# Attention, expert layer and feed-forward on one core: token lists kept in SBUF, a repriced schedule, grouped 64-token tails

## The chip, the core and the metric

One core of a Trainium2 chip runs the whole program in one launch. TensorE (PE, with its weight loads as PEld) does the matrix products, VectorE (DVE) and ScalarE (ACT) the elementwise work, GpSimd (POOL) elementwise work and the indirect DMAs, SyncE (SP) issues the plain DMAs. All DMAs share 16 DMA engines. The metric is the device time of one execution in microseconds (us), the median of three runs.

## The reference

Three stages follow each other. Every token goes to exactly one of 8 experts, 576 tokens each.

```python
# 1: attention without a token-by-token product, 8 batches, 8 heads, 576 tokens, 64 wide
q_s = softmax(q, axis=-1)              # over the 64 features
k_s = softmax(k, axis=2)               # over the 576 tokens
kv  = einsum('bhsd,bhse->bhde', k_s, v)
x   = einsum('bhsd,bhde->bhse', q_s, kv)    # -> (4608, 512)
# 2: experts; tokens are given out greedily by descending logit, at most 576 per expert
logits = x @ w_gate
out[mask_e] = relu(x[mask_e] @ w1[e]) @ w2[e]        # 512 -> 1024 -> 512
# 3: dense feed-forward, 512 -> 2048 -> 512
h = x @ w_in
y = (h * tanh(softplus(h))) @ w_out
```

## The kernel before, in words

**The planner.** Nothing here is ordered by hand. Every piece of work is given to `Sched.op` (L45) with its engine, an estimated cost, what it reads and writes, a priority (lower goes first) and the buffers it takes. `Sched.run` (L75) plays this forward and emits, again and again, the piece that could start first by those costs, ties going to the priority. What comes out is a fixed order of instructions on each engine; each engine works through its own in order, so an instruction that waits holds up everything behind it on that engine. There are four such plans: attention with the first routing, the expert phases, the last pieces of the last expert, and the feed-forward.

**Attention** (L137 to L479). Per batch, `k_side` takes the maximum of k over the tokens, POOL subtracts it (`sub`, `subh`) and ACT takes the exponential. `kv_side` multiplies k by v into one PSUM tile: `mm` (L295) runs, per head, four matmuls over 128 tokens (L304) and one over the last 64 (L308). `norm` (L312) sums two columns (L315), adds a small constant (L316), inverts and scales. `q_side` does the same for q, multiplies it with kv, forms the gate logits (L397 to L402), and scales x, mostly on POOL (`late`, L409). `store` writes x to the DRAM tensor `xd`.

**Routing** (`route`, L569, `round`, L774). For each expert in turn, six rounds of comparing on DVE (`cm`, L790) and counting on PE (`rt`, L798) find the threshold; `rows` writes the weight row numbers `wi`; `onehot` and `lists` then gather the 576 token numbers, and `ids` writes them to the SBUF tile `ix` (L755). `keep` (L760) copies them to a DRAM list `gl` with two DMAs of 4-byte elements (L763, L764). Much later `ldg` (L1278) reads all lists back as `gix`, by which the feed-forward scatters its output rows.

**Expert phases.** `load_x` (L877) gathers the tokens by `ix` with five indirect DMAs from POOL (`xg`, L883), PE transposes them (`tp`, `tpf`), ACT and DVE split them into a high and a low part `xT`. `load_expert` (L847) gathers the weights in eight indirect DMAs of 512 KB (`wst`, three buffers, L855), and ACT and DVE split each into two `unit` tiles (L836, L842). `expert` (L916) then runs 128 groups of three matmuls for `hp` (L925) and `yp` (L942) per expert. Interleaved are the routing of the next expert and `convert_w` (L997): 32 blocks of the feed-forward weights are read (SP), rebuilt (ACT, DVE) and written back to DRAM as `wd`. Its first seven blocks may start when the first list is known (L1050).

**Feed-forward** (L1104): `hp` (L1115) and `yp` (L1157) over nine chunks of 512 tokens.

Of the kernel before, what the change touches and what calls it, by code (L numbers as in the profile page):

```python
# [12 lines left out]
I32 = mybir.dt.int32  # L13
# [123 lines left out]
def attention(tc, nc, cst, q, k, v, w_gate, xs, L, R, xd, route):  # L137
# [27 lines left out]
    def load_k(b):  # L165
# [10 lines left out]
        for blk in range(2):  # L176
            sc.op("DMA", 1.46, lambda blk=blk: one_blk(blk), w=[("k", b, blk)] + ([("kk", b)] if blk == 0 else []),
                  new=[("k", ("kk", b))] if blk == 0 else [], prio=0)
        if b % 2 == 0:
            sc.op("DMA", 1.46, half, w=[("kh", b // 2)], new=[("kh", ("kh", b // 2))], prio=0)  # L180

    def load_v(b):
# [10 lines left out]
        for blk in range(2):  # L193
            sc.op("DMA", 1.46, lambda blk=blk: one_blk(blk), w=[("v", b, blk)] + ([("vv", b)] if blk == 0 else []),
                  new=[("v", ("vv", b))] if blk == 0 else [], prio=0)
        if b % 2 == 0:
            sc.op("DMA", 1.46, half, w=[("vh", b // 2)], new=[("vh", ("vh", b // 2))], prio=0)

    def load_q(b):
# [10 lines left out]
        for blk in range(2):  # L210
            sc.op("DMA", 1.46, lambda blk=blk: one_blk(blk), w=[("q", b, blk)], new=[("q", ("q", b, blk))], prio=0)
        if b % 2 == 1:
            sc.op("DMA", 1.46, half, w=[("q", b, 2)], new=[("qh", ("q", b, 2))], prio=0)


    def k_side(b):
# [58 lines left out]
        sc.op(DVE, 0.6, lambda: mx1(0), r=[("k", b, 0), kk], w=[km], new=[("km", km)], prio=p)  # L275
        sc.op(DVE, 1.2, lambda: mx1(1), r=[("k", b, 1), kk], w=[km], prio=p)
        sc.op(DVE, 0.6, mx2, r=[kh, km], w=[km, khx], prio=p)
        sc.op(PE, 0.45, tr, r=[km], w=[mT], new=[("mT", mT)], prio=p)
        sc.op(DVE, 0.65, red, r=[mT], w=[dg], new=[("dg", dg)], prio=p)
        sc.op(PE, 0.45, bc, r=[dg], w=[mb], new=[("mT", mb)], prio=p)  # L280
        sc.op(ACT, 0.5, cp, r=[mb], w=[ms], new=[("ms", ms)], prio=p)
        for blk in range(2):
            sc.op(POOL, 2.3, lambda blk=blk: sub(blk), r=[ms, kk, ("k", b, blk)], w=[("k", b, blk)], prio=p)
            sc.op(ACT, 0.95, lambda blk=blk: ex(blk), r=[kk], w=[("k", b, blk)], prio=p)
        sc.op(POOL, 1.2, subh, r=[ms, kh, khx], w=[khx], prio=p)
        sc.op(ACT, 0.52, exh, r=[kh], w=[khx], prio=p)


    def kv_side(b):
# [5 lines left out]
        def mm(h0, h1):  # L295
            if h0 == 0:
                T[kvp] = ps.tile([128, 4, 66], F32, name="kvp", tag="mT", bufs=2)
            pt = T[kvp]
            for h in range(h0, h1):
                a, i = h % 2, h // 2  # L300
                n = 0
                for blk in range(2):
                    for r in range(2):
                        nc.tensor.matmul(pt[a * 64:a * 64 + 64, i, r:r + 65], T["k", b, blk][:, h, r, :],  # L304
                                         T["v", b, blk][:, h, 65 * r:65 * r + 65],
                                         start=(h == a and n == 0), stop=False, skip_group_check=True)
                        n += 1
                nc.tensor.matmul(pt[a * 64:a * 64 + 64, i, 1:66], T["kh", b // 2][o:o + 64, h, :],  # L308
                                 T["vh", b // 2][o:o + 64, h, :], start=False, stop=(h >= 6),
                                 skip_group_check=True)  # L310
# [26 lines left out]
        def cpg():  # L337
            nc.scalar.activation(kv[:, :, 128:144], T[g], AF.Copy)

        kr = [("k", b, 0), ("k", b, 1), ("khx", b), ("kh", b // 2), ("kk", b), ("vv", b), ("v", b, 0),  # L340
              ("v", b, 1), ("vh", b // 2)]
        for h0 in range(0, 8, 4):
            sc.op(PE, 0.9, lambda h0=h0: mm(h0, h0 + 4), r=kr, w=[kvp],
                  new=[("mT", kvp)] if h0 == 0 else [], prio=p)
        sc.op(DVE, 1.3, norm, r=[kvp], w=[KVk], new=[("KV", KVk)], prio=p)
        sc.op(PE, 0.45, tr, r=[KVk], w=[kT], new=[("mT", kT)], prio=p)
        sc.op(ACT, 0.5, cp, r=[kT], w=[kTs], prio=p)
        sc.op(PE, 0.9, gate, r=[kTs], w=[g], new=[("mT", g)], prio=p)
        sc.op(ACT, 0.1, cpg, r=[g], w=[KVk], prio=p)


    def q_side(b):
# [78 lines left out]
        for u in range(2 + b % 2):  # L431
            n = 1 if u == 2 else 2
            qk, m, qe = ("q", b, u), ("qm", b, u), ("qe", b, u)
            sc.op(DVE, 0.06 + 0.53 * n, lambda u=u: mx(u), r=[qk], w=[m], prio=p)
            sc.op(POOL, 0.1 + 0.9 * n, lambda u=u: sub(u), r=[m], w=[qk], prio=p)
            sc.op(ACT, 0.1 + 0.43 * n, lambda u=u: ex(u), r=[qk], w=[qe], new=[("qe", qe)], prio=p)
            for r in range(n):
                qT, xp, x = ("qT", b, u, r), ("xp", b, u, r), ("x", b, u, r)
                sc.op(PE, 0.45, lambda u=u, r=r: tr(u, r), r=[qe], w=[qT], new=[("qT", qT)], prio=p)
                sc.op(ACT, 0.5, lambda u=u, r=r: cp(u, r), r=[qT], w=[x], prio=p)  # L440
                sc.op(PE, 1.0, lambda u=u, r=r: mm(u, r),
                      r=[x, ("KV", b)] + ([("KV", b - 1)] if u == 2 else []), w=[xp],
                      new=[("xp", xp)], prio=p)
                sc.op(DVE, 0.55, lambda u=u, r=r: logits(u, r), r=[xp], w=[("R", b, u, r), ("L", j_of(u) + r)],
                      prio=p + 3.11)
                if (j_of(u) + r) % 6 < 5 or b == 7 and u == 2:
                    sc.op(ACT, 0.5, lambda u=u, r=r: copy(u, r), r=[xp], w=[x], prio=p + 3.74)
                    sc.op(POOL, 1.25, lambda u=u, r=r: late(u, r), r=[("R", b, u, r)], w=[x], prio=1000)
                else:
                    sc.op(DVE, 0.62, lambda u=u, r=r: out(u, r), r=[xp, ("R", b, u, r)], w=[x], prio=p + 3.74)  # L450

            sc.op("DMA", 0.73 * n, lambda u=u: store(u), r=[("x", b, u, r) for r in range(n)], prio=3000)
# [106 lines left out]
class Moe:  # L559


    def __init__(self, tc, nc, c, L, sm):
# [770 lines left out]
```

## Time and profile before

| what | value |
|---|---|
| median of three runs | 1568.68 us (1568.53 to 1569.06) |
| the profiled execution: its time, its span | 1567.17 us, 1565.4 us |
| mean granted PE clock | 0.968 |
| busy: PE, DVE, ACT, POOL | 93%, 62%, 48%, 18% |
| DMA | 161.03 MB, mean 103 GB/s |

The span runs from the first to the last instruction that the profiler saw. PE is busy almost all the time, but that is a mean over stages: a table of stretches shows for each how long PE worked and which clock it was granted (1.00 is 2.4 GHz, 0.50 is 1.2 GHz). A timeline row gives the start, the duration, the instruction and, in brackets, how long the engine stood idle before it and what ended that. For a DMA the profile gives the time from its issue to its landing.

### The profile page before, as it was taken

The page shows a single profiled execution, that of the slowest core. Times are in us where ns is not written, and L with a number is a line of the kernel's source. Part 1 is how long each engine was busy: PE and PEld are TensorE (multiplying, and loading weights), DVE is VectorE, ACT ScalarE, POOL GpSimd, SP SyncE. Part 2 cuts the span into 40 slices and gives each one's busy share as a digit, 9 for nine tenths or more (in the row PEclk, how much of TensorE's full clock was granted, in tenths as well). Part 3 has the DMA queues.
Part 4 walks back from the last instruction along what each step waited for, and adds up shares of the span by engine and source line. Part 5 has one row for each costly group of instructions (what it writes and reads, how often), then busy time and mean ns, then how long its engine had stood idle before and what let it go on. Part 6 is the DMA issues. An engine that isn't in the chain of part 4 may idle for free.

```text
span 1565.4 us, 24440 instructions
## 1 busy us (share of the span) xinstructions
PE 1459.3 (93%) x9698; PEld 1269.4 (81%) x9698; DVE 968.2 (62%) x2017; ACT 747.2 (48%) x1334; POOL 284.2 (18%) x302
## 2 busy tenths in 40 slices
PE   5999539899999898999999999999999999999998
PEld 4888539789889798999988888888888888888886
DVE  6787668668666576772365655555555655555553
ACT  2655224224233334552465655556565655556553
POOL 7667431221330212110000101010000101010001
PEclk9999759999999899999999999999999999999999
DMA  9766464665552549863750100000010100000000
GB/s 243 208 174 196 150 152 135 140 165 168 127 151 73 167 118 251 277 245 100 261 183 1 48 7 34 21 27 27 8 48 0 43 13 34 21 28 14 3 26 27
DMA packets 122244, 161.03 MB, mean 103 GB/s; under 512 B 29969, under 2 KB 93457, under 8 KB 122129
## 3 DMA queue, kind: packets, MB, share of 16 engines
q1 hardware_dynamic: 107088, 107.03, 22.5%
q0 software_dynamic: 15040, 52.44, 12.0%
q8 instruction: 76, 1.25, 0.3%
q14 instruction: 40, 0.32, 0.1%
HBM read 114.33 MB, written 45.11 MB: 102 GB/s over the span
## 4 chain that ended last, share of the span: by engine, by line
PE 58%; issue 27%; DVE 5%; DMA 5%; POOL 2%; ACT 1%; SPq 0%; POOLq 0%; ACTq 0%; DVEq 0%
PE hp L925 12%; PE hp L1115 12%; PE yp L942 12%; PE yp L1157 11%; DMA wst<-in_moe_w_dram,wi 4%; PE rt L798 3%; PE kvp L304 2%; PE xp L387 2%; POOL out_dram L1169 1%; PE tp L894 1%; PE kvp L308 1%; DMA w<-in_moe_w_in_dram 1%; DVE cm L790 1%; DVE km L227 1%; POOL xg L883 0%
## 5 line engine op out<-in xcount | busy, mean ns | idle before, releaser
L1157 PE MATMUL yp<-unit,g 128*128 128x512 f32 x1728 | 421.0, 393 | 0.0
L1115 PE MATMUL hp<-yc,unit 128*128 128x512 f32 x1728 | 420.3, 393 | 0.0
L1157 PEld LDWEIGHTS yp<-unit,g 128*128 128x128 f32 x1728 | 324.6, 188 | 74.3
L1115 PEld LDWEIGHTS hp<-yc,unit 128*128 128x128 f32 x1728 | 324.4, 188 | 73.0
L925 PE MATMUL hp<-xT,unit 128*128 128x288 f32 x1536 | 287.4, 305 | 3.1 <-DVE hh L934 3.1
L942 PE MATMUL yp<-hh,unit 128*128 128x288 f32 x1536 | 276.4, 300 | 0.0
L1137 DVE SCALAR_TENSOR_TENSOR u<-w,r 128x512 f32<-128x512 f32 x144 | 99.6, 692 | 228.7 <-ACT r L1133 228.6
L925 PEld LDWEIGHTS hp<-xT,unit 128*128 128x128 f32 x1536 | 231.6, 193 | 5.0 <-DVE hh L934 3.3
L942 PEld LDWEIGHTS yp<-hh,unit 128*128 128x128 f32 x1536 | 229.2, 191 | 1.0 <-ACT ys L949 0.2
L1169 POOL DMA_INDIRECT out_dram<-os,gix x36 | 36.6, 1017 | 823.3 <-ACT os L1165 568.4
L930 ACT ACTIVATE hh<-hp 128x288 fp32r<-128x288 f32 x128 | 52.4, 409 | 232.0 <-PE hp L925 185.1
L1145 ACT ACTIVATE g<-w 128x512 fp32r<-128x512 f32 x144 | 90.5, 628 | 144.2 <-PE yp L1157 143.2
L1149 DVE TENSOR_TENSOR g<-w,g 128x512 fp32r<-128x512 f32 x144 | 99.3, 689 | 57.3 <-ACT g L1145 56.1
L1131 ACT ACTIVATE w<-u 128x512 f32<-128x512 f32 x144 | 90.8, 630 | 81.4 <-DVE g L1149 59.5
L934 DVE SCALAR_TENSOR_TENSOR hh<-hp,hh 128x288 fp32r<-128x288 f32 x128 | 58.3, 456 | 114.1 <-ACT hh L930 113.2
L1122 ACT ACTIVATE u<-hp 128x512 f32<-128x512 f32 x144 | 84.7, 588 | 91.3 <-PE hp L1115 90.6
L855 POOL DMA_INDIRECT wst<-in_moe_w_dram,wi x64 | 69.7, 1088 | 291.3 <-DVE unit L842 78.1
L836 ACT ACTIVATE unit<-wst 128x512 fp32r<-128x512 f32 x128 | 77.4, 645 | 84.9 <-DMA wst<-in_moe_w_dram,wi 76.8
L842 DVE TENSOR_TENSOR unit<-wst,unit 128x512 fp32r<-128x512 f32 x128 | 85.3, 684 | 36.1 <-ACT unit L836 35.9
L1138 DVE SCALAR_TENSOR_TENSOR r<-u,r 128x512 f32<-128x512 f32 x144 | 99.6, 692 | 4.9
L1141 DVE SCALAR_TENSOR_TENSOR w<-r,hp 128x512 f32<-128x512 f32 x144 | 97.9, 680 | 0.1
L798 PE MATMUL rt<-cm,C 128*8 128x32 bf16 (+1 forms) x1512 | 52.6, 187 | 44.3 <-DVE cm L790 37.0
(166 smaller groups left out, 1488.8 us busy)
## 6 DMA issues: line engine op xcount, KB each, us to landing
wd<-unit SPq DMA_DIRECT2D x32, 512.0 KB, 3.5
unit<-wd SPq DMA_DIRECT2D x32, 512.0 KB, 8.5
yd<-ys SPq DMA_DIRECT2D x16, 576.0 KB, 3.6
k<-in_k_dram SPq DMA_DIRECT2D x16, 512.0 KB, 5.8
q<-in_q_dram SPq DMA_DIRECT2D x16, 512.0 KB, 4.2
v<-in_v_dram SPq DMA_DIRECT2D x16, 512.0 KB, 6.5
xd<-xs SPq DMA_DIRECT2D x16, 512.0 KB, 3.3
w<-in_moe_w_in_dram SPq DMA_DIRECT2D x16, 512.0 KB, 5.5
```

The lines of the kernel that those rows point to most:

```text
L798: nc.tensor.matmul(T["c4"][0:E, 0:NT_], T["C"][:, j], T["cm"][:, j // 2, :, j % 2], start=(j == 0), stop=(j == NJ - 1))
L842: nc.vector.tensor_tensor(f, v, h, op=OP.subtract)
L925: MM(t, u[:, a, 128 * (f % 4):128 * (f % 4) + 128], x[:, b, k, HALF * hf:HALF * hf + HALF], start=(k == 0 and n == 0), stop=(k == 3 and n ...
L942: MM(T["yp", ph, hf][d], u[:, a, 128 * d:128 * d + 128], t[:, b], start=(f == 0 and n == 0), stop=(f == 7 and n == 2))
L1115: MM(t, u[:, a, 128 * (m % 4):128 * (m % 4) + 128], T["yc", c][:, b, k], start=(n == 0), stop=(n == 11))
L1131: nc.scalar.activation(w, T["u", c, m], AF.Square, bias=1.0)
L1137: V.scalar_tensor_tensor(e, w, 1.0, r, op0=OP.add, op1=OP.mult)
L1138: V.scalar_tensor_tensor(r, e, 2.0, r, op0=OP.subtract, op1=OP.mult)
L1141: V.scalar_tensor_tensor(T["w", c, m], T["r", c, m], 0.5, T["zp", c, m], op0=OP.add, op1=OP.mult)
L1145: nc.scalar.activation(g[:, 0], T["w", c, m], AF.Copy)
L1149: V.tensor_tensor(g[:, 1], T["w", c, m], g[:, 0].bitcast(F32), op=OP.subtract)
L1157: MM(T["op", c][t], g[:, a, 128 * t:128 * t + 128], u[:, b], start=(m == 0 and n == 0), stop=(m == 15 and n == 2))
```

## The change

- Lists: `keep` copies each list with two small POOL copies into the SBUF tile `gix`; the DRAM lists, their 16 stores and the four loads of `ldg` are gone.
- First expert: the token gathers and the w1 splits of expert 0 get priority -2000.
- The weight staging has four buffers instead of three; to make room, the one-hot tile `A` shares the buffer of `cm`, so the next routing's first compare follows the list matmuls.
- Tails: the eight 64-token matmuls of a batch stand together, as a piece of their own that alone waits for the 64-token part of k and v.
- `norm`: the constant is added first, on both PSUM columns, and the sum taken after.
- Conversion: the first seven weight blocks now wait for the third list (`("ix", 2 + n//7)`), the next seven for the fourth, and so on.
- Planner costs: most of attention's are raised, the token gather's latency is lowered from 10 to 5, the weight gather's raised to 5.5. These move the order everywhere.

```diff
-        sc.op(DVE, 0.6, lambda: mx1(0), r=[("k", b, 0), kk], w=[km], new=[("km", km)], prio=p)
+        sc.op(DVE, 1.4, lambda: mx1(0), r=[("k", b, 0), kk], w=[km], new=[("km", km)], prio=p)
...
-        def mm(h0, h1):
-            if h0 == 0:
+        def mm(h0, h1, tail):
+            if h0 == 0 and not tail:
...
+                if tail:
+                    nc.tensor.matmul(pt[c, i, 1:66], T["kh", b // 2][o:o + 64, h, :],
+                                     T["vh", b // 2][o:o + 64, h, :], start=False, stop=(h >= 6),
+                                     skip_group_check=True)
+                    continue
...
-            nc.vector.tensor_reduce(s, pt[:, :, 0:66:65], axis=AX, op=OP.add)
-            nc.vector.tensor_scalar(s, s, EPS, None, op0=OP.add)
+            s2 = wk.tile([128, 4, 2], F32, name="ks2")
+            nc.vector.tensor_scalar(s2, pt[:, :, 0:66:65], EPS / 2, None, op0=OP.add)
+            nc.vector.tensor_reduce(s, s2, axis=AX, op=OP.add)
...
-            nc.sync.dma_start(gl[o:o + 512, :].rearrange("(q p) o -> p (q o)", p=128), ix[:, 0:4])
-            nc.sync.dma_start(gl[o + 512:o + CAP, :], ix[0:64, 4:5])
-        sc.op("DMA", 1.5, keep, r=[("ix", ph)], w=[("gl", ph)], prio=p)
+            if ph % 2:
+                nc.gpsimd.tensor_copy(g[64:128, at + 4:at + 9], ix[0:64, 0:5])
+                nc.gpsimd.tensor_copy(g[0:64, at + 5:at + 9], ix[64:128, 0:4])
+            else:
+                nc.gpsimd.tensor_copy(g[:, at:at + 4], ix[:, 0:4])
+                nc.gpsimd.tensor_copy(g[0:64, at + 4:at + 5], ix[0:64, 4:5])
+        sc.op("POOL", 0.3, keep, r=[("ix", ph)], w=[("gl", ph)], prio=0)
...
-            t = T[which, ph, g] = self.ld.tile([128, 1024], F32, name="wst", bufs=3)
+            t = T[which, ph, g] = self.ld.tile([128, 1024], F32, name="wst", bufs=4)
...
-                    self.split(key, src_of, unit, p + g)
+                    self.split(key, src_of, unit, -2000 + g if first else p + g)
...
-        p = 100 * ph - 89.16
+        p = 100 * ph - 89.16 if ph else -2000
...
-            sc.op("DMA", 2.6, ld, r=[("ix", 0 + n // 7)], w=[k64], new=[("w64", k64)], prio=p)
+            sc.op("DMA", 2.6, ld, r=[("ix", 2 + n // 7)], w=[k64], new=[("w64", k64)], prio=p)
...
-    def ldg():
-        for i in range(E // 2):
-            nc.sync.dma_start(gix[:, 9 * i:9 * i + 9], gl[i].rearrange("(t p) o -> p (t o)", p=128))
-    sc.op("DMA", 2.0, ldg, w=["gix"], prio=2000)
```

The order on POOL, from the last scaling of x to the gathers of the second expert, before and then after the change (`wst` are weight gathers, `xg` token gathers):

```order
L409 TENSOR_TENSOR xs<-xs,R 128x512 x24
L855 DMA wst<-in_moe_w_dram,wi 128x1024 x3
L883 DMA xg<-xd,ix 128x512 x4
L855 DMA wst<-in_moe_w_dram,wi 128x1024
L883 DMA xg<-xd,ix 64x512
L855 DMA wst<-in_moe_w_dram,wi 128x1024 x7
L883 DMA xg<-xd,ix 128x512 x4
```

```order
L411 TENSOR_TENSOR xs<-xs,R 128x512 x9
L768 COPY gix<-ix 128x4
L769 COPY gix<-ix 64x1
L888 DMA xg<-xd,ix 128x512 x4
L860 DMA wst<-in_moe_w_dram,wi 128x1024 x4
L888 DMA xg<-xd,ix 64x512
L860 DMA wst<-in_moe_w_dram,wi 128x1024 x9
```

The three weight gathers that stood ahead of the first list now stand behind it, behind two copies and four token gathers.

On PE, around the first batch's product of k and v (`kvp`), before and after:

```order
L237 MATMUL mT<-ident,km 128x128 x4
L246 MATMUL mb<-ident,mx 128x128 x4
L304 MATMUL kvp<-v_0_218,k_256 64x65 x2
L304 MATMUL kvp<-v_1_219,k_258 64x65 x2
L308 MATMUL kvp<-vh_224,kh 64x65
```

```order
L309 MATMUL kvp<-v_0_215,k_253 64x65 x2
L309 MATMUL kvp<-v_1_216,k_255 64x65 x2
L376 MATMUL qT<-ident,qe 128x128 x4
L303 MATMUL kvp<-vh_221,kh 64x65 x8
L376 MATMUL qT<-ident,qe 128x128 x12
L328 MATMUL kT<-ident,KV_223 128x128 x4
```

Before, a tail matmul follows each four of the others; now all eight of a batch come in one row, after all 32 others.

On SP, from the last stores of x on, before and after:

```order
L763 DMA gl_101<-ix 128x4x1
L764 DMA gl_101<-ix 64x1
L1014 DMA w_2269<-in_moe_w_in_dram 128x1024
L1014 DMA w_2282<-in_moe_w_in_dram 128x1024
L1014 DMA w_2514<-in_moe_w_in_dram 128x1024
L1048 DMA wd_69<-unit 128x1024
```

```order
L424 DMA xd<-xs 128x1024 x4
L428 DMA xd<-xs 64x512 x2
L957 DMA yd_61<-ys 128x4x288 x2
L1019 DMA w_3981<-in_moe_w_in_dram 128x1024
L1019 DMA w_4043<-in_moe_w_in_dram 128x1024
L957 DMA yd_62<-ys 128x4x288
```

The list stores are gone, and the first conversion loads stand behind both result stores of the first expert.

## Rows read from the trace of the kernel before

**Rows 1.** Table of stretches; PE, PEld, DVE, ACT, POOL busy (instructions), PE clock, DMA.

```profile
0.00:176.40 176.40, 146.15 (x1266) 126.37 (x1267) 132.56 (x298) 84.75 (x135) 125.72 (x125) 0.98 0.75 211
176.40:231.90 55.50, 19.07 (x339) 16.33 (x337) 32.62 (x102) 8.14 (x15) 15.91 (x14) 0.53 0.49 120
231.90:761.50 529.60, 497.67 (x4644) 477.98 (x4644) 340.18 (x848) 193.78 (x414) 101.68 (x93) 0.97 0.56 162
761.50:1565.40 803.90, 796.43 (x3457) 648.74 (x3455) 462.86 (x770) 460.51 (x772) 40.87 (x71) 1.00 0.11 39
```

**Rows 2.** DMA issues of the whole span: count, KB each, median us to landing.

```profile
xg<-xd,ix POOLq DMA_INDIRECT x40, 11.4
...
yst<-yd SPq DMA_DIRECT2D x8, 32.0 KB, 2.2
gl<-ix SPq DMA_DIRECT2D x8, 2.0 KB, 11.8
```

**Rows 3.** DMA of 448 to 460 us, around the fifth list store.

```profile
DMA packets 690, 0.30 MB, mean 25 GB/s; under 512 B 618, under 2 KB 618, under 8 KB 689
```

**Rows 4.** SP's timeline: the second list store.

```profile
271.41 0.38 SPq L763 DMA_DIRECT2D gl<-ix  x1
```

**Rows 5.** DVE's timeline behind it.

```profile
292.50 0.69 DVE L842 TENSOR_TENSOR unit<-wst,unit 128x512 fp32r<-128x512 f32 x1 [6.26 <-ACT unit L836]
```

**Rows 6.** PE's timeline: a wait behind that store, and the two that follow none.

```profile
246.03 1.05 PE L798 MATMUL rt<-cm,C 128*8 128x32 bf16 x36 [1.23 <-DVE cm L790]
...
294.88 1.12 PE L798 MATMUL rt<-cm,C 128*8 128x32 bf16 x36 [4.89 <-DVE cm L790]
...
660.56 0.66 PE L894 MATMUL tp<-ident,xg 128*128 128x128 f32 x4 [1.72 <-DVE xT L904]
```

**Rows 7.** PE's waits, 231.9 to 761.5 us: us in total, times, longest.

```profile
PE rt L798 <- DVE cm L790: 15.2, 4, 4.9
PE rt L798 <- issue: 6.6, 8, 2.7
```

**Rows 8.** Table of stretches behind two of the stores, and one undisturbed.

```profile
290.00:300.00 10.00, 5.12 (x55) 4.77 (x55) 6.67 (x16) 4.78 (x9) 2.16 (x2) 0.66 0.48 169
...
355.00:391.00 36.00, 36.00 (x370) 34.38 (x371) 29.69 (x87) 16.26 (x34) 5.32 (x5) 1.00 0.49 162
...
523.00:545.00 22.00, 15.71 (x166) 14.56 (x166) 10.24 (x27) 7.96 (x17) 2.27 (x2) 0.77 0.71 258
```

**Rows 9.** POOL's timeline, first gathers of the first expert.

```profile
199.62 1.18 POOL L855 DMA_INDIRECT wst<-in_moe_w_dram,wi  x1 [20.65 <-DVE rk L670]
...
205.44 0.95 POOL L883 DMA_INDIRECT xg<-xd,ix  x1 [1.61 <-DVE ix L755]
...
210.92 1.57 POOL L855 DMA_INDIRECT wst<-in_moe_w_dram,wi  x1 [0.30 <-issue]
```

**Rows 10.** Line L855, the 64 weight gathers: time from issue to landing.

```profile
DMA to landing us min/median/max: 4.2/5.4/14.1
```

**Rows 11.** ACT's timeline: the first expert's w1 split in its first staging buffer.

```profile
203.95 1.21 ACT L836 ACTIVATE unit<-wst 128x512 fp32r<-128x512 f32 x2 [26.10 <-DMA wst<-in_moe_w_dram,wi]
```

**Rows 12.** PE's timeline, first transpose and first product of the first expert.

```profile
219.26 1.12 PE L894 MATMUL tpf<-ident,xg 128*128 128x128 f32 x4 [4.95 <-DMA xg<-xd,ix]
...
231.88 4.62 PE L925 MATMUL hp<-xT,unit 128*128 128x288 f32 x24
```

**Rows 13.** PE's groups in attention, 0 to 176.4 us: count, busy us, mean ns.

```profile
L304 PE MATMUL kvp<-v,k 128*64 128x65 f32 x512 | 47.1, 239 | 0.0
...
L308 PE MATMUL kvp<-vh,kh 64*64 64x65 f32 x128 | 22.1, 255 | 0.1
```

**Rows 14.** DVE's groups in attention, 0 to 178 us.

```profile
L397 DVE TENSOR_SCALAR R<-xp 128x8 f32<-128x8 f32 x36 | 5.8, 162 | 17.9 <-PE xp L387 16.6 <-PE xp L390 0.8 <-ACT xs L417 0.3
...
L316 DVE TENSOR_SCALAR ks<-ks 128x4 f32<-128x4 f32 x8 | 5.0, 620 | 0.3
```

**Rows 15.** POOL's groups: its small copies.

```profile
L467 POOL COPY wgbd<-wg 64x32 f32<-64x32 f32 x2 | 0.4, 204 | 0.1
```

More of the change, by code (lines that the diff above doesn't have):

```diff
@@ L210, in load_q @@
         for blk in range(2):
-            sc.op("DMA", 1.46, lambda blk=blk: one_blk(blk), w=[("q", b, blk)], new=[("q", ("q", b, blk))], prio=0)
+            sc.op("DMA", 1.8, lambda blk=blk: one_blk(blk), w=[("q", b, blk)], new=[("q", ("q", b, blk))], prio=0)
         if b % 2 == 1:
-            sc.op("DMA", 1.46, half, w=[("q", b, 2)], new=[("qh", ("q", b, 2))], prio=0)
+            sc.op("DMA", 0.95, half, w=[("q", b, 2)], new=[("qh", ("q", b, 2))], prio=0)
     def k_side(b):
@@ L433, in q_side @@
             qk, m, qe = ("q", b, u), ("qm", b, u), ("qe", b, u)
-            sc.op(DVE, 0.06 + 0.53 * n, lambda u=u: mx(u), r=[qk], w=[m], prio=p)
-            sc.op(POOL, 0.1 + 0.9 * n, lambda u=u: sub(u), r=[m], w=[qk], prio=p)
-            sc.op(ACT, 0.1 + 0.43 * n, lambda u=u: ex(u), r=[qk], w=[qe], new=[("qe", qe)], prio=p)
+            sc.op(DVE, 0.16 + 0.54 * n, lambda u=u: mx(u), r=[qk], w=[m], prio=p)
+            sc.op(POOL, 0.4 + 0.8 * n, lambda u=u: sub(u), r=[m], w=[qk], prio=p)
+            sc.op(ACT, 0.2 + 0.45 * n, lambda u=u: ex(u), r=[qk], w=[qe], new=[("qe", qe)], prio=p)
@@ L442, in q_side @@
+                sc.op(PE, 1.04, lambda u=u, r=r: mm(u, r),
                       r=[x, ("KV", b)] + ([("KV", b - 1)] if u == 2 else []), w=[xp],
                       new=[("xp", xp)], prio=p)
-                sc.op(DVE, 0.55, lambda u=u, r=r: logits(u, r), r=[xp], w=[("R", b, u, r), ("L", j_of(u) + r)],
+                sc.op(DVE, 1.0, lambda u=u, r=r: logits(u, r), r=[xp], w=[("R", b, u, r), ("L", j_of(u) + r)],
                       prio=p + 3.11)
                 if (j_of(u) + r) % 6 < 5 or b == 7 and u == 2:
-                    sc.op(ACT, 0.5, lambda u=u, r=r: copy(u, r), r=[xp], w=[x], prio=p + 3.74)
-                    sc.op(POOL, 1.25, lambda u=u, r=r: late(u, r), r=[("R", b, u, r)], w=[x], prio=1000)
-                else:
-                    sc.op(DVE, 0.62, lambda u=u, r=r: out(u, r), r=[xp, ("R", b, u, r)], w=[x], prio=p + 3.74)
@@ L452, in q_side @@
-            sc.op("DMA", 0.73 * n, lambda u=u: store(u), r=[("x", b, u, r) for r in range(n)], prio=3000)
+                    sc.op(ACT, 0.62, lambda u=u, r=r: copy(u, r), r=[xp], w=[x], prio=p + 3.74)
+                    sc.op(POOL, 1.1, lambda u=u, r=r: late(u, r), r=[("R", b, u, r)], w=[x], prio=1000)
+                else:
+                    sc.op(DVE, 0.71, lambda u=u, r=r: out(u, r), r=[xp, ("R", b, u, r)], w=[x], prio=p + 3.74)
+            sc.op("DMA", 0.9 * n, lambda u=u: store(u), r=[("x", b, u, r) for r in range(n)], prio=3000)
@@ L1229, in attention_moe_ffn @@
     wd = [dr.tile([128, 1024], F32, name=f"wd{i}") for i in range(32)]
-    gl = [dr.tile([2 * CAP, 1], I32, name=f"gl{i}") for i in range(E // 2)]
     ctx.enter_context(tc.manual_schedule())
```

86 lines of the change are left out of this document (40 added, 46 removed).

## The prediction

> **What bounds the kernel now.** I read the table of stretches first. Its four rows [rows 1] are attention (0 to 176.4 us), the first routing and the loading of the first expert (to 231.9), the expert phases (to 761.5) and the feed-forward. In the last PE works 796.43 of 803.90 us at full clock, and the change touches nothing in it but the source of the scatter indices: its time stays. In the expert phases PE stands idle for 529.60 - 497.67 = 31.9 us; in the second stretch it works only 19.07 of 55.50 us, at a clock of 0.53; in attention it works 146.15 of 176.40.
>
> Next the DMA issues [rows 2]. A list store of 2.0 KB takes 11.8 us to land, five times as long as a 32 KB load (2.2). It is written in 4-byte elements, and around one of them 618 of 690 packets are under 512 B while all engines together move 25 GB/s [rows 3], against a mean of 162 in the expert phases [rows 1]. The token gathers, which start at the same moment since they wait for the same list, land after 11.4 us [rows 2].
>
> Then the chain behind such a store. The second is issued at 271.41 [rows 4]. A weight gather issued behind it comes late, ACT's split waits for it, DVE's split of it waits 6.26 us for ACT [rows 5], and DVE's next routing compare stands behind that split. So PE waits 4.89 us for the compare at 294.88 [rows 6]. The list of PE's waits [rows 7] is led by this pattern (15.2 us) and by waits that the profile can't name, "issue" (6.6 us), which all begin 9 to 14 us behind a list store. Of the waits over 0.5 us, two follow no store within 30 us: 1.23 us at 246.03 and 1.72 at 660.56 [rows 6]. The clock falls after the waits: 0.66 from 290 to 300 us, 0.77 from 523 to 545 [rows 8].
>
> **The change, part by part.** The sum is made against the profiled span of 1565.4 us; the median of the runs, 1568.68, is 3.3 us above it, and that is added at the end. A measurement of this kernel can't tell less than about 0.2%, 3 us, from no change.
>
> *List stores.* 31.9 us of idle less the two unrelated waits (2.95) leaves 29.0 us that can go. I take 24, since a later expert's work will sometimes run into the next wait, on DVE. Bounds: 29, and 6 if only the 6.6 us of "issue" go. The low clock goes with them. A mean of 0.97 over 529.60 us is 15.9 us of full-speed work not granted [rows 1], part of it while PE was idle anyway. From 290 to 300 us the clock was low for 2 x 0.34 x 10 = 6.8 us, of which at most 4.9 were idle, so at least 1.0 us of work was lost and at most 3.4; from 523 to 545 us the same reckoning gives 1.9 to 5.1 [rows 8]. I take half, 8 us; bounds 3 and 15. The four loads of the lists stood beside a fully busy PE at the end of the expert phases and give nothing.
>
> *The copies.* Two POOL copies per list, each about the 204 ns of POOL's other small copies [rows 15], plus 0.3 us of issue for each: 1.0 us ahead of each set of token gathers. For experts 1 to 7 this lies under PE's work on the expert before; without that cover it would cost 7 us. For the first expert it is on the path, counted next.
>
> *First expert.* The list is ready just before 205.44 [rows 9], unchanged relative to the end of attention. Before, three weight gathers went out from 199.62 and were split from 203.95 on [rows 11], the fourth only at 210.92 [rows 9], behind the store; it took the 14.1 us of the slowest one [rows 10] and was split at about 227. The token gathers landed late too: first transpose at 219.26, first product at 231.88 [rows 12]. Now all four weight gathers stand behind the list, which is a loss of the 5.8 us from 199.62 to 205.44 taken alone. The four token gathers go out from 206.4, at a pitch of (210.92 - 205.44) / 4 = 1.37 us; the weights from 211.9 to 216.0. With the median landing of 5.4 us [rows 10] the tokens are in SBUF by 216, the last weight at 221.4, and its two splits (1.21 us on ACT [rows 11], 0.69 behind it on DVE [rows 5]) end at 223.3. PE can start on the first weights at about 218.5 and has done the first eight groups of three (24 matmuls, 4.62 us before, at 236.5) at about 224.5: 12 us earlier. The fourth staging buffer lets w2 follow as soon as the first w1 split is done, at about 219.5: it is ready at about 227, where PE wants it at 226. So 11 us. Bounds: 14, if landings take 4.2 us and nothing stutters; 5, if they take the 11.4 us of the token gathers before, which puts the last split at 229.3 and the eight groups at 231.
>
> *Tails.* The eight tails of a batch run as 128 instructions, 22.1 us, 173 ns each; the other 512 take 47.1 us, 92 ns each [rows 13]. No row shows a row of tails, so the bounds are 0 and, at 92 ns each, 22.1 - 11.8 = 10.3 us. I take the middle, 5: PE is the busiest engine in attention, but DVE at 132.56 of 176.40 us [rows 1] is near enough to take some back. The Trainium skill (TensorEngine Tiling (Array Packing), Key Properties) says that a change of the tiling mode drains TensorE. By that rule nearly the whole surcharge is the switch, the term would be 10 and the forecast 1517.
>
> *`norm`.* The sum on SBUF took 620 ns (L316), the like one from PSUM takes 162 (L397) [rows 14]: 8 x 0.46 = 3.7 us of DVE, of which PE waited for little; I take 1 (0 to 4).
>
> *Attention's order.* With dearer costs the planner runs the k side ahead and moves late q loads on SP behind stores of x. PE's idle there is 30.2 us [rows 1], much of it the start, which keeps its order. I take 0; bounds 10 us either way, a third of that idle.
>
> *Conversion.* The 32 blocks are the same work, now begun in the third phase and finished nearer the end of the last expert. It frees DVE in the first phases, where it hid; near the end DVE must do it beside a full PE. I take 2 us lost for a new wait somewhere (0 to 10).
>
> Sum: -24 - 8 - 11 - 5 - 1 + 2 = -47. 1565.4 - 47 + 3.3 = **1521.7 us**, so 1522.
>
> **The rivals.** *(a) Forecast: the list stores are the common cause.* For it: all the chains above. Its own range is 1503 to 1537. Chance 0.75.
>
> *(b) DVE takes over the bound.* Where nothing disturbs it DVE already works 29.69 of 36 us [rows 8], and the later conversions add to the later phases. In-order, a compare for the routing then waits behind splits, and PE behind it. If half of the waits and of the lost clock come back, the terms are -12 - 4 - 11 - 6 + 2 = -31, 1538 us. Against it: over the whole of the expert phases DVE works 340.18 of 529.60 us [rows 1]. Chance 0.17.
>
> *(c) Slower: the gathers are slow for another reason and stay so.* If POOL's gathers land late because DVE's work keeps POOL from making them, not because of the stores, the expert phases gain nothing, and all four w1 gathers now start after the list. That gives away the 5.8 us of head start that the first three had [rows 9]: at 14.1 us each [rows 10] the first lands at 226.0 and the fourth at 230.1. With the copies' 7 us uncovered and no gain in attention, the time is 1568.7 + 5.8 + 7 = 1582. It decides if gathers with no store in flight take over 10 us. Against it: the gather of 199.62, issued while DVE built the list, was in its split at 203.95 [rows 9, 11]. The Trainium skill (SBUF — State Buffer, section SBUF: two separate sides) does state this mechanism: GpSimd can't write its descriptors while certain DVE operations hold the shared port. Chance 0.05.
>
> That the change doesn't do what it says is out for the stores: the order shows none on SP. What is left, 0.03, is a gain given back in attention or at the start of the feed-forward so that little changes.
>
> **How the numbers follow.** 1522 is case (a). The best ends together, -29 - 15 - 14 - 10 - 4, give 1497; I stop at 1503, where most of them hold. On the other side (b) with 10 us lost in attention is 1548. So 1503 to 1548 for 8 in 10. Faster: (a), (b) and a third of the rest, 0.93; the same 0.02; slower 0.05.
>
> **What would show it.** Right: weight and token gathers land in 4 to 7 us throughout; PE's idle in the expert phases is under 12 us and "issue" is gone from its waits; the first product comes about 13 us after the first list; the tails' mean falls towards 92 ns; attention ends within 10 us of 176.4. Wrong: DVE compares still hold PE for over 10 us in sum (b); gathers still take over 10 us (c); a wait of PE for `yc` or `unit` at the start of the feed-forward, which would put the loss in the conversion; attention ending later than 180.

## The result, and the profile after

The kernel before took 1568.87 us (median; 1568.53 to 1570.27), the changed kernel 1514.18 us (1512.70 to 1517.17): ratio 0.9641, 95% interval 0.9617 to 0.9665. It is 55 us faster, where 47 were forecast, and lies inside the range of 1503 to 1548. The profiled execution took 1513.42 us, its span is 1511.6.

The table of stretches of the changed kernel, cut at the same events as [rows 1] (end of attention, first product, first matmul of the feed-forward); the columns are those of [rows 1]:

```profile
0.00:159.00 159.00, 120.10 (x1267) 108.37 (x1268) 133.31 (x298) 85.47 (x135) 129.09 (x124) 0.91 0.83 232
159.00:203.50 44.50, 16.47 (x300) 14.11 (x300) 24.67 (x88) 3.18 (x7) 11.40 (x13) 0.58 0.31 98
203.50:707.60 504.10, 492.92 (x4679) 472.77 (x4680) 348.52 (x862) 199.31 (x423) 106.99 (x110) 0.99 0.52 175
707.60:1511.60 804.00, 796.57 (x3458) 648.53 (x3456) 462.88 (x770) 460.62 (x772) 40.87 (x71) 1.00 0.11 39
```

Subtract stretch by stretch. Attention gave 17.4 us, the way to the first product 11.0, the expert phases 25.5, the feed-forward nothing. The sum, 53.8, is the difference of the spans. PE's idle in the expert phases fell from 31.9 to 11.2 us, and its busy time by 4.8 us as the clock rose from 0.97 to 0.99.

PE's waits of the changed kernel in the expert phases (us in total, times, longest), against [rows 7]:

```profile
PE rt L815 <- DVE fl L810: 3.0, 1, 3.0
PE rt L803 <- issue: 2.8, 4, 1.2
PE rt L815 <- issue: 1.5, 2, 1.3
PE rt L803 <- DVE cm L795: 1.3, 2, 1.1
```

The wait for the routing compares, 15.2 us in [rows 7], is 1.3 now. Of "issue", 4.3 us stay in these rows: the forecast said that it would go.

PE's groups in attention, changed kernel, for [rows 13] (busy us, then the mean duration in ns):

```profile
L309 PE MATMUL kvp<-v,k 128*64 128x65 f32 x512 | 26.5, 242 | 0.5 <-ACT k L266 0.5
L303 PE MATMUL kvp<-vh,kh 64*64 64x65 f32 x128 | 5.9, 236 | 0.0
```

Divide the busy time by the count: a tail instruction costs 46 ns where it cost 173, and one of the main products 52 where it cost 92. The two groups may not be added, though: in the kernel before their records overlap, since each tail stands between main products. Here is `kvp` taken as one tile, before and then after (after the length of the stretch: PE, PEld, DVE):

```profile
0.00:176.40 176.40, 61.28 (x640) 50.62 (x640) 8.05 (x24) 0.98 0.75 211
0.00:159.00 159.00, 32.45 (x640) 29.28 (x640) 8.04 (x24) 0.91 0.83 232
```

So PE has 28.8 us less to do for these products. All its work in attention fell by 26.0 us, from 146.15 to 120.10, at a clock of 0.91 where it was 0.98; attention shows 17.4 of it.

POOL's timeline, the first expert's steps (compare [rows 9]), and PE's up to the first product (compare [rows 12]):

```profile
187.68 0.34 POOL L768 COPY gix<-ix 128x4 int32<-128x4 int32 x1 [26.14 <-DVE ix L757]
187.97 0.18 POOL L769 COPY gix<-ix 64x1 int32<-64x1 int32 x1
188.77 1.24 POOL L888 DMA_INDIRECT xg<-xd,ix  x1 [0.62 <-issue]
...
194.18 0.94 POOL L860 DMA_INDIRECT wst<-in_moe_w_dram,wi  x1 [0.30 <-issue]
```

```profile
192.35 1.09 PE L899 MATMUL tpf<-ident,xg 128*128 128x128 f32 x4 [5.14 <-DMA xg<-xd,ix]
...
201.31 0.18 PE L815 MATMUL rt<-dg,n 8*128 8x8 bf16 x1 [4.25 <-issue]
...
203.47 2.58 PE L930 MATMUL hp<-xT,unit 128*128 128x288 f32 x6 [0.93 <-ACT unit L841]
...
206.59 4.30 PE L930 MATMUL hp<-xT,unit 128*128 128x288 f32 x18
```

The copies take 1.1 us up to the first gather, as forecast, and the first transpose comes 3.6 us behind its gather's issue. Then 4.25 us pass in which PE waits for nothing that the profile names, and the last transposes stand behind them. DVE stood still in the same time: the matmul at 201.31 needs the count that DVE's `fl` makes, and that starts only at 201.03, after 6.12 us that the profile puts down to "remote", something outside the engines that it doesn't name:

```profile
201.03 0.21 DVE L810 TENSOR_SCALAR_CACHE_REDUCE fl<-rt 8x64 bf16<-8x64 f32 x1 [6.12 <-remote]
```

### The profile page after: what moved, and what is told of

Read it like the earlier page. It is cut to its first block, busy times and chain, and to the rows that moved or that the text cites. A ratio compares the mean times of both kernels' runs of the same rounds, so it can differ in the third digit from the quotient of the medians.

```text
span 1511.6 us, 24413 instructions
## 1 busy us (share of the span) xinstructions
PE 1426.1 (94%) x9698; PEld 1243.8 (82%) x9698; DVE 969.4 (64%) x2017; ACT 748.6 (50%) x1334; POOL 288.4 (19%) x318
## 3 DMA queue, kind: packets, MB, share of 16 engines
q1 hardware_dynamic: 97552, 106.99, 22.1%
## 4 chain that ended last, share of the span: by engine, by line
PE 58%; issue 30%; DVE 5%; DMA 3%; POOL 2%; SPq 1%; ACT 1%; another core or an unknown queue 0%; POOLq 0%; ACTq 0%; DVEq 0%
PE hp L930 13%; PE hp L1120 13%; PE yp L947 13%; PE yp L1162 12%; PE rt L803 3%; POOL out_dram L1174 2%; PE xp L389 1%; PE tp L899 1%; DMA k<-in_k_dram 1%; DVE km L227 1%; PE kvp L309 1%; DMA wst<-in_moe_w_dram,wi 1%; DMA w<-in_moe_w_out_dram 1%; DMA v<-in_v_dram 0%; DVE qm L360 0%
## 5 line engine op out<-in xcount | busy, mean ns | idle before, releaser
L947 PE MATMUL yp<-hh,unit 128*128 128x288 f32 x1536 | 269.8, 297 | 0.2 <-issue 0.2
L930 PEld LDWEIGHTS hp<-xT,unit 128*128 128x128 f32 x1536 | 228.5, 191 | 5.0 <-ACT unit L841 1.3
L947 PEld LDWEIGHTS yp<-hh,unit 128*128 128x128 f32 x1536 | 225.6, 189 | 1.1 <-issue 0.4
L860 POOL DMA_INDIRECT wst<-in_moe_w_dram,wi x64 | 66.5, 1039 | 237.9 <-DVE L L774 56.1
L1137 ACT ACTIVATE r<-w 128x512 f32<-128x512 f32 x144 | 91.1, 633 | 4.6
L1138 ACT ACTIVATE r<-r 128x512 f32<-128x512 f32 x144 | 91.0, 632 | 4.6
```

The lines of the kernel that those rows point to most:

```text
L930: MM(t, u[:, a, 128 * (f % 4):128 * (f % 4) + 128], x[:, b, k, HALF * hf:HALF * hf + HALF], start=(k == 0 and n == 0), stop=(k == 3 and n ...
L947: MM(T["yp", ph, hf][d], u[:, a, 128 * d:128 * d + 128], t[:, b], start=(f == 0 and n == 0), stop=(f == 7 and n == 2))
L1137: nc.scalar.activation(r, w, AF.Ln, bias=1.0)
L1138: nc.scalar.activation(r, r, AF.Exp, scale=-1.0)
```

## The experiments

The results of the experiments name the chip that a kernel ran on; I call them A, B and C (that of the first two rows is not on record). Kernels that share a letter also shared the runs of the kernel before, but for "the same again", which has its own. The stages are those of one execution, the profiled one, in us, and it lies up to 5.6 us from the median; the feed-forward takes 804.0 to 804.2 in all of them and is left out.

| run | chip | attention ends | to first product | expert phases | median us | ratio to before, 95% interval |
|---|---|---|---|---|---|---|
| before | - | 176.4 | 55.5 | 529.5 | 1568.87 | |
| changed | - | 159.0 | 44.5 | 504.1 | 1514.18 | 0.9641 (0.9617 to 0.9665) |
| lists alone | A | 176.0 | 51.0 | 496.8 | 1533.68 | 0.9779 (0.9736 to 0.9822) |
| dead stores | A | 157.6 | 48.8 | 556.3 | 1567.71 | 0.9973 (0.9954 to 0.9992) |
| dead rows | A | 156.7 | 44.4 | 503.7 | 1512.91 | 0.9642 (0.9604 to 0.9680) |
| tails alone | A | 171.9 | 56.3 | 532.0 | 1566.11 | 0.9977 (0.9955 to 0.9998) |
| tails undone | B | 182.7 | 44.3 | 506.0 | 1538.99 | 0.9795 (0.9777 to 0.9813) |
| first expert undone | B | 157.2 | 49.6 | 522.3 | 1535.36 | 0.9781 (0.9758 to 0.9804) |
| three buffers | B | 161.2 | 43.1 | 519.5 | 1524.87 | 0.9701 (0.9681 to 0.9721) |
| early weights, new order | B | 160.6 | 41.1 | 534.7 | 1536.65 | 0.9771 (0.9746 to 0.9796) |
| early weights, same order | C | 161.6 | 39.9 | 489.1 | 1496.06 | 0.9544 (0.9531 to 0.9557) |
| the same again | B | 156.6 | 39.4 | 502.5 | 1506.33 | 0.9604 (0.9584 to 0.9625) |
| lists and attention | C | 161.2 | 50.8 | 488.0 | 1504.77 | 0.9596 (0.9579 to 0.9614) |
| the same, list's copies later | C | 156.5 | 46.9 | 485.1 | 1498.79 | 0.9567 (0.9553 to 0.9581) |

Ten of these executions have the changed kernel's attention, instruction for instruction, and it ends between 156.5 and 161.6. So a difference of 5 us there, between single executions, means nothing.

**Are the list stores the cause?** First the kernel before with the lists in SBUF and nothing else:

```
-            nc.sync.dma_start(gl[o:o + 512, :].rearrange(...), ix[:, 0:4])
-            nc.sync.dma_start(gl[o + 512:o + CAP, :], ix[0:64, 4:5])
+            nc.gpsimd.tensor_copy(g[:, at:at + 4], ix[:, 0:4])
+            nc.gpsimd.tensor_copy(g[0:64, at + 4:at + 5], ix[0:64, 4:5])
...
-    sc.op("DMA", 2.0, ldg, w=["gix"], prio=2000)
```

> The kernel before with one edit: lists copied on POOL into the SBUF tile, no list stores, no reload ahead of the feed-forward; three staging buffers, old priorities and latencies. Theory (the 4-byte list stores fill the DMA engines and make gathers, splits and instruction reads late): the expert phases fall from 529.6 us to 500 to 512, PE idle in them from 31.9 to under 16, the kernel to 1541 to 1556. Rival (the fourth buffer, the first expert's priority and the new latencies gain the time): the phases stay within 5 us of 529.6, the kernel at 1563 to 1569.

The expert phases, in the table of stretches:

```profile
227.00:723.80 496.80, 486.98 (x4644) 469.75 (x4644) 340.15 (x848) 194.78 (x414) 100.51 (x107) 0.99 0.52 172
```

They fell by 32.8 us, 22.1 of idle (9.8 are left) and 10.7 of busy time: the two terms of the forecast, 24 and 8, with no fourth buffer and no new latency. The kernel came out 7 us below the theory's range. But the planner wrote a new order here too: from 293 us of the kernel before on, DVE works in another order. The clean test holds the order fixed. It is the reverse, the changed kernel with dead stores, in the old form, beside its copies:

```
             ix, g, at = self.T["ix", ph], self.gix, 9 * (ph // 2)
+            nc.sync.dma_start(d[o:o + 512, :].rearrange("(q p) o -> p (q o)", p=128), ix[:, 0:4])
+            nc.sync.dma_start(d[o + 512:o + CAP, :], ix[0:64, 4:5])
```

> The changed kernel with one addition: each list is also stored to DRAM as 576 elements of 4 bytes on the SP queue, in the form the kernel before had, to a place that nothing reads; orders of PE, DVE, ACT and POOL are those of the changed kernel, instruction for instruction. Theory (the stores' small packets clog the DMA engines): stalls of 2 to 5 us come back behind each of the eight lists, the expert phases grow from 504 to 522 to 532 us, the kernel to 1530 to 1545. Rival (order, buffer and latencies made the gain): phases within 4 us of 504, the kernel at 1512 to 1519.

And the same with whole rows of the list, 20 bytes each:

```
+            nc.sync.dma_start(self.dead[ph], ix)
```

> As the run with dead list stores, at the same places of the SP queue, but each list goes out as 128 rows of 20 bytes: fewer than a quarter of the elements. If the number of elements sets the loss, the phases grow by a fifth to a third of what the 4-byte stores cost (some 4 to 7 us, the kernel at 1518 to 1522); if any small store behind the list costs the same (the wait of SP for the list, or the queue), by the same 18 us or more, to 1530 or over; if neither does, 1512 to 1517.

On PE, DVE, ACT and POOL both have the changed kernel's order, row for row. The 4-byte stores cost more than the theory had it: the whole gain is gone, 52 us of it in the phases alone, while the rows of 20 bytes cost nothing that can be measured. The DMA of the 12 us from a store on, first with dead stores (452 to 464 us), then with dead rows (426 to 438):

```profile
DMA packets 681, 0.30 MB, mean 25 GB/s; under 512 B 608, under 2 KB 608, under 8 KB 681
```

```profile
DMA packets 792, 2.24 MB, mean 186 GB/s; under 512 B 251, under 2 KB 251, under 8 KB 790
```

The first is [rows 3] over again. What it does to the run with dead stores, in the timelines of SP, POOL and PE:

```profile
452.13 0.37 SPq L766 DMA_DIRECT2D gl<-ix  x1
```

```profile
453.23 1.12 POOL L892 DMA_INDIRECT xg<-xd,ix  x1
```

```profile
466.91 1.11 PE L903 MATMUL tp<-ident,xg 128*128 128x128 f32 x4 [6.88 <-DMA xg<-xd,ix]
```

The gather is issued 1.1 us behind the store, and PE gets its rows 13.7 us later, having stood idle for 6.9. Its sum over the expert phases, from PE's waits:

```profile
PE tp L903 <- DMA xg<-xd,ix: 32.8, 6, 6.9
```

This may also be why the stores hurt more here than in the kernel before, whose phases took 530 us with the same stores. The changed planner counts 5.0 us for such a gather where the old one counted 10, and the transposes stand early in its order: PE begins to wait for them 6.8 us behind the first gather's issue. In the kernel before, whose gather was issued at 449.12, it began 11.9 us behind, and waited little:

```profile
461.57 0.66 PE L894 MATMUL tp<-ident,xg 128*128 128x128 f32 x4 [0.58 <-DMA xg<-xd,ix]
```

With the stores in flight the planner's old figure of 10 fits better: the shorter latency does not make the gathers faster, it needs them to be. No run changes the latency alone, so this is argued.

**Attention: the grouping, or the new costs?** The grouping alone, in the kernel before, with its old costs and normalisation:

```
-                nc.tensor.matmul(pt[...], T["kh", b // 2][...], T["vh", b // 2][...], ...)
...
+        sc.op(PE, 0.2, lambda: mm(0, 8, True), r=[("khx", b), ("kh", b // 2), ("vh", b // 2)], w=[kvp], prio=p)
```

> The kernel before with one edit: the eight tail matmuls of a batch come in one group behind its 32 main ones; every cost in the planner's table stays as it was, the normalisation too. Theory (each change between a 128-row and a 64-row product delays both neighbours): the main products fall from 92 to about 52 ns, the tails from 173 to about 46 ns, and attention ends at 160 to 168 us (before: 176.4), the kernel at 1553 to 1561. Rival (the gain of the changed kernel's attention is its repriced order, the grouping alone is worth the tails' own 5 us or less): attention ends at 171 to 177 us, the kernel at 1563 to 1569.

PE's groups and, below, its two largest waits in this attention:

```profile
L309 PE MATMUL kvp<-v,k 128*64 128x65 f32 x512 | 25.1, 232 | 0.0
L303 PE MATMUL kvp<-vh,kh 64*64 64x65 f32 x128 | 5.5, 224 | 0.0
```

```profile
PE kT L327 <- DVE KV L321: 17.9, 6, 7.1
PE mT L237 <- DVE km L231: 17.7, 4, 10.1
```

The mechanism is right; the time is the rival's. The surcharge went from both neighbours of each switch, and `kvp` as one tile takes 30.5 us of PE where it took 61.3:

```profile
0.00:171.90 171.90, 30.54 (x640) 27.42 (x640) 8.02 (x24) 0.90 0.77 216
```

But attention became only 4.5 us shorter: PE now waits for DVE's normalisation in six places, 17.9 us in all where it was 2.6. Then the counter-piece (the 36 us of PE in its text are the two groups' sum, which counts their overlap twice; it is 30.7), the changed kernel without the grouping:

```
-        sc.op(PE, 0.9, lambda: mm(0, 8, True), r=[("khx", b), ("kh", b // 2), ("vh", b // 2)], w=[kvp], prio=p)
+            sc.op(PE, 2.45, lambda h0=h0: mm(h0, h0 + 4), r=kr, w=[kvp], ...)
```

> The changed kernel with one part undone: each head's tail product stands behind its four main ones again (two planner operations of 2.45 us); the new costs of all other operations stay. The grouping alone in the kernel before brought attention from 176.4 to 171.9 us (4.6 of PE's 36 us). Theory (grouping and repricing add up, so repricing is the other 13 us): attention ends at 161 to 166 us, the kernel at 1516 to 1522. Rival (they need each other: only with the new order is PE waited for, so that its 36 us count): attention ends at 168 to 177, the kernel at 1522 to 1532. Second rival (repricing did it all): attention within 1.5 us of 159, the kernel at 1512 to 1516.

```profile
0.00:182.70 182.70, 153.87 (x1267) 135.50 (x1268) 131.87 (x298) 85.60 (x135) 127.97 (x124) 0.86 0.71 202
```

Grouping alone takes 4.5 us off attention, the new costs alone add 6.3, both together take off 17.4: the rival's reading, and beyond its range. With the new costs and ungrouped tails PE is the busiest engine, 153.9 of 182.7 us; with the old costs and grouped tails DVE is, 140.9 of 171.9. Two limits: 4.5 and 6.3 us are single executions, and about as large as the spread of 5 us above; and in each of the two runs the planner wrote an attention order of its own, with PE's clock at 0.90 and 0.86 where the kernel before had 0.98. The two together give far more than the sum of these, by more than that spread; what each is worth alone, with the order held, was not measured.

**The other parts.** Three of them taken back or moved one at a time:

```
-                    self.split(key, src_of, unit, -2000 + g if first else p + g)
+                    self.split(key, src_of, unit, p + g)
...
-        p = 100 * ph - 89.16 if ph else -2000
+        p = 100 * ph - 89.16
```

> The changed kernel with one part undone: the first expert's gathers of x and its splits have the priorities of the kernel before again. Theory (an earlier first product shortens the kernel by as much): first product 5 to 11 us later than 203.5, the kernel at 1519 to 1526. Rival (the lead is given back, because from there on PE has the same work to do in order and runs at a lower clock after its long idle stretch, as the kernel before with nothing but the lists in SBUF took 547.7 us from the end of attention to the feed-forward against 548.6 here): first product later, but those two stages together within 3 us of 548.6 and the kernel at 1511 to 1518.

```
-            t = T[which, ph, g] = self.ld.tile([128, 1024], F32, name="wst", bufs=4)
+            t = T[which, ph, g] = self.ld.tile([128, 1024], F32, name="wst", bufs=3)
```

> The changed kernel with three weight staging buffers in place of four, in the pool and in the planner. Theory (the fourth buffer takes waits out of the gathers and splits): PE idle in the expert phases grows from 11 us by 4 or more, the kernel at 1518 to 1525. Rival (three are enough once the list stores are gone, as in the kernel before with nothing but the lists in SBUF, whose PE idled 9.8 us in these phases): within 3 us of 1514.

```
-                      new=[("wst", key)], prio=-2000 if first else p, lat=5.5)
+                      new=[("wst", key)], prio=-2002 if first else p, lat=5.5)
...
+    sc.op("POOL", 0.0, m.keep0, r=[("ix", 0)], w=[("gl", 0)], prio=-2001)
```

> The changed kernel with POOL's first steps exchanged: the four gathers of the first expert's w1 rows, which need its number alone, stand ahead of the copies of the first list and of the gathers of x, which need the list. If the weights' landing sets the first product, it comes at 194 to 199 us after a like attention (203.5 now), and the kernel, if that lead counts, at 1505 to 1511; if the lead is given back as between the other two kernels, 1512 to 1516; if the copies behind the four gathers make the list's gathers late instead, the first product comes at 204 or later and the kernel at 1515 or over.

All three lost 11 to 23 us against the changed kernel's 1514, most of it in the expert phases. The first lies outside every range that I had given; the third has the time of a case whose condition, a first product at 204 or later, it doesn't meet (201.7). Each has a wait of PE at another place. One row from each, in this order, a part of the loss only:

```profile
PE hp L930 <- DVE unit L847: 8.6, 2, 8.2
```

```profile
PE tp L899 <- DVE cv L1033: 5.0, 1, 5.0
```

```profile
PE hp L933 <- DVE unit L850: 6.2, 1, 6.2
```

The last kernel was to gain: its first product came 41.1 us behind attention, where the changed kernel's came after 44.5. Yet its phases are 31 us longer. So the question became whether a new order costs this, rather than the part that was edited. The planner is greedy: one number changed early can reorder every engine for the 500 us behind it. To take that out I moved the same four gathers by hand, after the planner had set its order. On PE, DVE, ACT and SP every row stands where the changed kernel has it:

```
+            if ph == t == 0:
+                for f in self.early:
+                    f()
+                self.keep0()
             x = T["xg", ph, t] = self.ld.tile([128, DM], F32, name="xg", bufs=4)
...
+            self.early = [lambda g=g: weight("w1", g, w1r) for g in range(4)]
```

> The changed kernel with nothing moved but POOL's first ten steps: the four gathers of the first expert's w1 rows stand ahead of the list's copies and the gathers of x; the order on PE, DVE, ACT and SP is the changed kernel's, row for row (the run with early weights let the planner write a new order for everything behind them). Theory (that run lost its 25 us to the new order, not to the early gathers): the expert phases stay at 501 to 507 us; the first product comes at 198 to 202 where it was 203.5, and the kernel at 1509 to 1513, or at 1513 to 1516 if the splits' place in ACT's and DVE's order gives the lead back. Rival (gathers that fly beside the list's work make the x gathers and instruction reads late): the first product at 204 or later, the kernel at 1516 or over.

Beside it ran the kernel before with lists and attention changed and none of the other parts, and the same with the first list's copies behind three weight gathers:

```
+            if ph == t == 0:
+                self.keep0()
```

> The kernel before with its lists in SBUF and the changed kernel's whole attention (grouped tails, new costs, new normalisation), and nothing else of the change: three staging buffers, old priorities, latencies and date of the conversions. Theory (those four parts earn nothing together, the lists and attention are the whole gain): attention ends at 157 to 161 us, then 545 to 551 us to the feed-forward, the kernel at 1509 to 1516. Rival (they earn what was lost when one of them alone was undone, 10 to 20 us): the kernel at 1520 to 1535.

> As the mixed run, with the first list's two copies put behind the three weight gathers that the old order already has ahead of the gathers of x, so that these gathers run 5 us earlier; no other row on any engine moves. If the start of the x gathers sets the first product, it comes 3 to 5 us earlier than in the mixed run and the kernel is 2 to 5 us faster, 1505 to 1513; if PE's work behind it gives the lead back, within 1.5 us of the mixed run.

The expert phases of these three, in that order:

```profile
201.50:690.60 489.10, 486.48 (x4679) 467.55 (x4680) 349.59 (x862) 200.41 (x423) 105.36 (x110) 1.00 0.54 180
```

```profile
212.00:700.00 488.00, 484.24 (x4643) 467.25 (x4643) 341.16 (x848) 194.35 (x414) 104.25 (x107) 1.00 0.52 175
```

```profile
203.40:688.50 485.10, 482.78 (x4644) 465.94 (x4645) 340.91 (x848) 194.37 (x414) 103.88 (x107) 1.00 0.53 177
```

All three beat the changed kernel's 1514.18 by 9 us or more, and every one by more than expected: PE is idle 2 to 4 us in its phases and the clock stays at 1.00. But the second of them has the expert code of the run with the lists alone, which idled 9.8 us on chip A. So the first kernel ran once more, unedited, and by chance on another chip:

> The kernel with the changed kernel's order and only POOL's first steps moved, once more, without any edit, because the three runs that it was compared among show no issue waits on DVE and PE at all in the expert phases (14 us on DVE in the changed kernel, its phases 504 us) and one of them has the same expert code as the run with nothing but the lists in SBUF, which does. Theory (the moved gathers take the waits away): again no issue waits, phases 487 to 491 us, the kernel at 1494 to 1499. Rival (the waits belong to the chip on which a kernel happens to run, not to the kernel): some 10 us of such waits on DVE, phases 500 to 506, the kernel at 1507 to 1514.

```profile
196.00:698.50 502.50, 490.54 (x4680) 470.68 (x4681) 349.15 (x862) 199.95 (x423) 106.73 (x110) 0.99 0.52 175
```

The rival's figures came true: 13.4 us in the phases lie between two executions of the same program on chips B and C. DVE's waits on B show what C doesn't have:

```profile
DVE fl L813 <- remote: 7.1, 2, 3.6
DVE hh L948 <- issue: 1.6, 2, 1.1
DVE xT L918 <- issue: 1.6, 2, 1.2
```

From this, three comparisons within a chip. On B the early weights with the changed order give 1506.33, with a rewritten order 1536.65: the new order alone costs 30 us. On C, from the end of attention to the feed-forward, early weights in the changed order take 529.0 us, lists and attention alone 538.8, and with the later copies 532.0. So priority, fourth buffer, latencies and conversion date together bring at most some 3 us once the gathers stand well, none of it in the phases, and the kernels' ranges overlap (1495.02 to 1496.42, 1494.28 to 1500.19). In the runs on B with the priorities or the fourth buffer undone the phases were 20 and 17 us longer than the changed order's 502.5; but on C both undone together, with the latencies and the date of the conversions, have phases of 488.0 against 489.1. So those losses are most likely the price of the orders that came out, not of the parts. Shown it is for the early weights alone, where the order was held; the two others were not run in the changed order, and "remote" waits of `fl`, 16.4 and 11.7 us in their phases against 7.1, are a part of their loss that the order need not explain.

**A faster version.** The early weights in the changed order took 1496.06 us on C and 1506.33 on B, against 1514.18 for the changed kernel and 1512.91 for the run with dead rows, which has the same order (chip A). The changed kernel is not known to have run on B or C, so the safe part is the stretch up to the first product: 39.9 and 39.4 us instead of 44.5 and 44.4. PE's timeline on B, where 4.25 us of "issue" stood:

```profile
190.60 1.09 PE L908 MATMUL tpf<-ident,xg 128*128 128x128 f32 x4 [5.83 <-DMA xg<-xd,ix]
...
194.61 0.17 PE L818 MATMUL rt<-dg,n 8*128 8x8 bf16 x1
...
195.96 0.40 PE L939 MATMUL hp<-xT,unit 128*128 128x288 f32 x1 [0.59 <-ACT unit L844]
```

And DVE's `fl`, which started at 201.03 after 6.12 us of "remote":

```profile
193.69 0.21 DVE L813 TENSOR_SCALAR_CACHE_REDUCE fl<-rt 8x64 bf16<-8x64 f32 x1 [0.52 <-PE rt L806]
```

The first transpose comes no earlier, 34.0 us behind attention against 33.4. The gain lies behind it, where this standstill is gone. The changed kernel, dead rows, tails undone and three buffers all have it at this place, 5.3 to 6.9 us long, two of them on B; the two executions with the gathers moved by hand, one of them on B, don't. How the gathers' place bears on it, and what the head start of the weights would be worth without it, stays open.

## Why the prediction was right, and where not

**List stores, clock** (-24 and -8, with +2 for the conversions: -30 in the expert phases). Measured -25.5 (20.7 of idle, 4.8 of busy time), and -32.8 with the lists alone. Right in cause and size, and case (a) of the rivals is shown with the order held: put 4-byte stores back and 52 us come back, put rows back and nothing does. The place of the wait is not the forecast's, though: behind the stores put back, PE waits 32.8 us for the token gathers and 1.1 for the compares. That "issue" would be gone was wrong in the changed kernel and on A and B; such waits have a second source. What the later conversions cost was not measured apart.

**Rival (b), DVE as the bound**, did not come: 1.3 us of waits for compares, not over 10. **Rival (c)**, gathers slow because of DVE: with no 4-byte store in flight the x gathers land sooner. Their line in the run with early weights in the same order, on C (for the changed kernel the profile has no such line), against 11.4 us in [rows 2]:

```profile
DMA to landing us min/median/max: 3.2/4.2/7.6
```

The Trainium skill's rule that GpSimd can't write its descriptors while certain DVE operations hold the port (SBUF — State Buffer, section SBUF: two separate sides) is not contradicted by that; it just is not what made these gathers late.

**First expert** (-11): measured -11.0, and that is luck. The working counted to the end of the first eight groups, 12 us earlier, and had the first product 13.4 earlier and 13 behind the list. The first product came 11.0 earlier and 15.8 behind the list, and the eight groups end 51.9 us behind attention where it was 60.1: 8.2 earlier. The standstill of 4.25 us on PE was in no term. I put the gain down to priorities and the fourth buffer, too. The lists alone brought 4.5 of it, and most of the lead that the other parts won was given back in the phases (from the end of attention to the feed-forward the changed kernel takes 548.6 us, the lists alone 547.8, though not known to be on one chip; on C 3 us are left of 7). I also took the loss of the three weight gathers' head start as part of the price; with all four early the stretch is about 5 us shorter, as the standstill goes with them.

**Tails** (-5) and **attention's order** (0): the steps that failed, 6 us forecast with the normalisation, 17.4 measured; the sign that attention ends within 10 us of 176.4 did not hold. The bound of 10.3 us for the tails was wrong because I took 92 ns as a main product's plain price, while some 40 of that were the switch, too; PE's saving was 28.8 us, not at most 10. The rule of the Trainium skill that I weighed there (TensorEngine Tiling (Array Packing), Key Properties: a change of mode drains TensorE) was the better guide, and the trace agrees; here the surcharge stands in the records on either side of the switch, 92 to 52 ns and 173 to 46. And the two terms don't add: -4.5 and +6.3 apart, -17.4 together.

**Normalisation** (-1): the addition of the constant, on both PSUM columns now, takes 160 ns where it took 620 on the four sums (L316 in [rows 14]), as forecast; its share of attention was not measured apart.

```profile
L316 DVE TENSOR_SCALAR ks<-kvp 128x8 f32<-128x8 f32 x8 | 1.3, 160 | 3.7 <-PE kvp L303 3.7
```

**The total** came within 7 us of the forecast because two errors have opposite signs: attention gave 11 us more than its terms, the expert phases 4.5 less.

## What to carry to other kernels

A store of single 4-byte elements is dear for everyone else on the DMA engines: look at the packets behind it, and write rows. When a mode switch recurs, price it on both neighbours, and ask which engine ends the stage before and after. With a greedy planner, test a part with the order held fixed: the one part tested both ways lost 30 us to the order that it happened to draw.

## What was not expected of the hardware

The same program took 1496.06 us on one chip and 1506.33 on another, with ranges that don't meet (1495.02 to 1496.42, 1504.26 to 1510.54), though the kernel before differed by under 0.3% between the three chips (1567.21 to 1571.68). The difference is in the expert phases: waits of DVE, ACT and PE that the profile doesn't name, and a clock of 0.99 against 1.00. Whether it belongs to the chip or to where a program's instructions lie in its memory stays open; so does what ends a "remote" wait. A comparison of kernels that differ by 1% needs both on one chip.
